# Second products turned to tokens x model columns, expert probabilities applied at the sum, one turn through DRAM

## The chip, the cores and the metric

The kernel runs on one core of a Trainium2 chip. The metric is the device time of one execution in microseconds (us). Before the change the median of three runs is 619.43 us (618.59 to 619.71).

## The reference

Three blocks follow each other: attention with a window (half the heads with a dilated one), a mixture of four experts in which every token uses every expert, and a feed-forward block with a sigmoid gate.

```python
# attention, out: x [1152 tokens, 512]
p = domain_probs / (domain_probs.sum(-1, keepdims=True) + 1e-09)
out = np.zeros((N, D))
for e in range(4):                       # w1[e] 512 x 1024, w2[e] 1024 x 512
    h = np.maximum(x @ w1[e], 0.0)
    out += p[:, e:e + 1] * (h @ w2[e])
x = out
h = x @ w_in                             # 512 x 2048
g = h * (1.0 / (1.0 + np.exp(-1.702 * h)))
return g @ w_out                         # 2048 x 512
```

All inputs and the result are float32.

## The kernel before

Products are run on TensorE (PE) in split precision: each operand is held as a high part and a low part (`xh`, `xl`; `wh`, `wl`), and a product is three matmuls: high x high, high x low, low x high. A matmul takes a stationary operand of 128 x 128 and a moving one of up to 512 columns, and adds into a PSUM bank of 128 x 512 float32. There are eight banks: four of the pool `ps`, four of the pool `pacc`.

The first expert is interleaved with attention by a table of words, SCRIPT. It works in three pieces of 384 tokens and eight tiles f of 128 hidden columns. `F` words are first products (`g1_part`, L521), `h` and `l` write the hidden tile's high and low part, and `2 f i` is a second product (`second`, L563): model columns i x 384 tokens, w2 stationary, the hidden tile moving, 4 values of i with three matmuls each. At f = 7 the sum is multiplied by the expert's probability and goes to `acc` (`g2`, L577), which is laid out model columns x tokens. The probabilities lie along the tokens there, so they have to be repeated on all 128 partitions: `p_turn` (L483) turns them on PE, stores them in DRAM (`pd`) and loads them back with a broadcast.

The other three experts and the gated block run in units s of 256 hidden columns (s = 4 to 15 the experts, 16 to 23 the gated block), each for two groups of tokens c (512 and 640 tokens). `first2` (L790) makes the hidden tile from seven products by a 2 x 2 scheme: the banks a, c, b, d get a product each, then a, c, d a second one. VectorE (DVE) forms `u` and `s` from b and d (L822, L824); the second product into d may start only when L824 has read it. For an expert, DVE then takes the larger of 0 and the value times the probability (`shared`, L839), ScalarE (ACT) writes the high part (L842) and DVE the low part (L852). `second_moe` (L887) is the second product: model columns x tokens, w2 stationary, hidden tile moving; four tiles of 512 tokens for c = 0 (24 matmuls) and eight of 320 tokens for c = 1 (48 matmuls), one DVE add into `acc` each (L919). Units 14 and 15 of c = 1 share one such pass. `second2` (L926), for the gated block, has the other orientation: tokens x model columns, the hidden tile stationary and w2 moving with 512 columns, 24 and 30 matmuls, and a multiply-add on DVE per tile (L946).

The order of units is: first products of (s, 0), second products of (s - 1, 1), first products of (s, 1), second products of (s, 0), and so on. Inside them a table, MID, says which background step is called at each of the places between products. Among these are the rounds that convert the gated block's weights: load a piece `sd` (L727), two ACT steps (L737, L738), two DVE steps into `m` (L743, L747), a GpSimd (POOL) add (L748), and a store of `m` to DRAM (L753). `m` has two buffers, so L743 of a round needs the store of two rounds ago to have landed; `sd` has three. The loads of the weights (`st`, L189) are background steps too. All DMAs are issued by SyncE (SP) in the order of the program: one that has to wait holds all behind it. DVE, ACT, POOL and PE also work in the order of the program.

## Time and profile before

| | |
|---|---|
| median of three runs | 619.43 us |
| the profiled execution's own time | 616.77 us |
| its span | 614.9 us |
| PE busy | 607.6 us, 99% |
| DVE busy | 472.9 us, 77% |
| POOL busy | 358.8 us, 58% |
| ACT busy | 275.9 us, 45% |

The profile is of one execution. The span runs from its first to its last instruction; the execution's own time is 1.9 us longer. Busy time of PE includes the tail of each matmul that overlaps the next one, so what PE does per matmul is read from the starts of matmuls that follow each other, not from the mean duration. An idle engine that nobody waits for costs nothing.

### The profile page before, as it was taken

To read this page: it belongs to the slowest core of one execution; us is meant where nothing else is said; L and a number is where in the kernel's file an instruction comes from. 1 tells how busy PE (TensorE), PEld (TensorE's weight loads), DVE (VectorE), ACT (ScalarE), POOL (GpSimd) and SP (SyncE) were. 2 spreads that over 40 slices of the span, in tenths; PEclk is the share of its full clock that TensorE was granted. 3 is DMA by queue.
4 is the path that set the end of the run, shared out by engine and by line. 5 is a ranking of instruction groups with operands and counts; after the bars stand their busy time and mean duration, and the time that the engine had idled before them with its cause. 6 is when DMAs were issued, how large, how long until landed. Compare 5 with 4: busy or idle time off the path is not lost.

```text
span 614.9 us, 11210 instructions
## 1 busy us (share of the span) xinstructions
PE 607.6 (99%) x4144; PEld 569.2 (93%) x4144; DVE 472.9 (77%) x994; ACT 275.9 (45%) x615; POOL 358.8 (58%) x334
## 2 busy tenths in 40 slices
...
GB/s 319 301 203 154 105 165 177 1 49 122 172 141 134 148 188 151 168 108 170 121 170 176 139 105 170 35 90 72 62 2 103 35 69 36 34 1 1 1 1 154
DMA packets 31446, 69.98 MB, mean 114 GB/s; under 512 B 6908, under 2 KB 12192, under 8 KB 31392
## 3 DMA queue, kind: packets, MB, share of 16 engines
...
q8 instruction: 32, 0.52, 0.4%
...
HBM read 56.26 MB, written 12.99 MB: 113 GB/s over the span
## 4 chain that ended last, share of the span: by engine, by line
PE 93%; DVE 3%; ACT 2%; DMA 1%; issue 1%; SPq 0%; DVEq 0%; ACTq 0%
PE gd L805 10%; PE gc L805 10%; PE ga L805 10%; PE g L539 8%; PE q L909 8%; PE q L911 8%; PE q L910 8%; PE q L939 5%; PE q L937 5%; PE q L938 5%; PE gb L805 5%; PE pa L573 3%; PE pa L575 3%; PE pa L574 3%; DMA pT01small<-home01small 1%
## 5 line engine op out<-in xcount | busy, mean ns | idle before, releaser
L909 PE MATMUL q<-h,w2l 128*128 128x320 f32 (+1 forms) x288 | 97.3, 338 | 0.1
L911 PE MATMUL q<-h,w2h 128*128 128x320 f32 (+1 forms) x288 | 97.2, 338 | 0.0
L910 PE MATMUL q<-h,w2h 128*128 128x320 f32 (+1 forms) x288 | 97.2, 337 | 0.0
L852 DVE TENSOR_TENSOR h<-cc,h 128x256 fp32r<-128x256 f32 (+1 forms) x80 | 74.0, 925 | 20.2 <-ACT h L842 12.5
L748 POOL TENSOR_TENSOR m<-m,sd 128x512 int32<-128x512 int32 x32 | 49.1, 1533 | 62.2 <-ACT h L842 36.8
L692 POOL TENSOR_TENSOR wsl<-ss,wsh 128x512 fp32r<-128x512 f32 x39 | 59.5, 1531 | 31.1 <-ACT wsh L691 31.1
L919 DVE TENSOR_TENSOR acc<-q,acc 128x512 f32<-128x512 f32 (+1 forms) x132 | 70.2, 546 | 9.6 <-PE q L911 8.5
L842 ACT ACTIVATE h<-cc 128x256 fp32r<-128x256 f32 (+3 forms) x48 | 33.0, 687 | 97.3 <-DVE cc L839 96.9
L827 POOL TENSOR_TENSOR cc<-s,u 128x256 f32<-128x256 f32 (+1 forms) x38 | 33.5, 882 | 59.9 <-DVE s L824 59.9
L911 PEld LDWEIGHTS q<-h,w2h 128*128 128x128 f32 x288 | 54.1, 188 | 4.4
L909 PEld LDWEIGHTS q<-h,w2l 128*128 128x128 f32 x288 | 54.1, 188 | 4.0 <-DVE acc L919 0.3
L910 PEld LDWEIGHTS q<-h,w2h 128*128 128x128 f32 x288 | 54.1, 188 | 3.9
L703 POOL TENSOR_TENSOR w2l<-st,w2h 128x512 fp32r<-128x512 f32 x37 | 54.1, 1475 | 5.3 <-ACT w2h L702 4.9
L939 PE MATMUL q<-w2h,h 128*128 128x512 f32 (+1 forms) x146 | 56.9, 390 | 0.0
L937 PE MATMUL q<-w2h,h 128*128 128x512 f32 (+1 forms) x146 | 56.7, 389 | 0.0
L938 PE MATMUL q<-w2l,h 128*128 128x512 f32 (+1 forms) x146 | 56.6, 388 | 0.0
L946 DVE SCALAR_TENSOR_TENSOR acc<-q,acc 128x512 f32<-128x512 f32 (+1 forms) x64 | 42.5, 677 | 11.5 <-PE q L939 11.1
L688 POOL TENSOR_TENSOR wal<-st,wah 128x512 fp32r<-128x512 f32 (+1 forms) x38 | 47.1, 1244 | 2.3 <-ACT wah L687 2.3
L805 PE MATMUL ga<-xh,wal 128*128 128x256 f32 (+1 forms) x160 | 47.3, 296 | 0.0
L805 PE MATMUL ga<-xl,wah 128*128 128x256 f32 (+1 forms) x160 | 47.3, 296 | 0.0
L805 PE MATMUL ga<-xh,wah 128*128 128x256 f32 (+1 forms) x160 | 47.2, 295 | 0.0
L839 DVE SCALAR_TENSOR_TENSOR cc<-cc,pb 128x256 f32<-128x256 f32 (+3 forms) x48 | 42.3, 882 | 1.0
...
## 6 DMA issues: line engine op xcount, KB each, us to landing
...
```

What stands on the lines that cost most here:

```text
L539: nc.tensor.matmul(pt[:, :C], w[:, kt, fs], xx[:, kt, c * C:(c + 1) * C], start=first and y == 0, stop=not todo and y == len(products[x]) - 1)
L692: fns.append(lambda x=x, dst=dst: engine(f"p.{s}.{x}").tensor_tensor(out=sl[:, dst], in0=sums[:, dst], in1=sh[:, dst].bitcast(F32), op=ALU ...
L703: fns.append(lambda o=o: engine(f"q.{s}.{2 * o + 1}").tensor_tensor(out=lo[:, o], in0=t[:, o], in1=hi[:, o].bitcast(F32), op=ALU.subtract))
L805: nc.tensor.matmul(bank_[:, :n], wz[:, y, m, :], xz, start=start and m == 0 and z == 0, stop=m == 1 and z == 2, skip_group_check=not start)
L852: nc.vector.tensor_tensor(out=hl[:, sub], in0=cc[:, sub], in1=hh[:, sub].bitcast(F32), op=ALU.subtract)
L909: nc.tensor.matmul(pt, wl[:, o, cols], hi, start=first, stop=False, skip_group_check=both)
L910: nc.tensor.matmul(pt, wh[:, o, cols], hi, start=False, stop=False, skip_group_check=both)
L911: nc.tensor.matmul(pt, wh[:, o, cols], lo, start=False, stop=last, skip_group_check=both)
L919: nc.vector.tensor_tensor(out=dst[:, on], in0=pt[:, on], in1=src[:, on], op=ALU.add)
L937: nc.tensor.matmul(pt, hi, wh[:, o, cols], start=o == 0, stop=False)
L938: nc.tensor.matmul(pt, hi, wl[:, o, cols], start=False, stop=False)
L939: nc.tensor.matmul(pt, lo, wh[:, o, cols], start=False, stop=o == 1)
```

## The change

The second products of the first expert and of units 4 to 13 get the orientation of `second2`: tokens x model columns, hidden tile stationary, w2 moving with 512 columns (`second`, `second_rows`). A tile of 128 tokens then has its probability on its own partition, so it is a factor per partition in the DVE step that adds to `acc` (or that writes it, for the first expert), and `shared` falls away for units 4 to 13; ACT writes the high part directly with Relu, and DVE the low part with a maximum and a subtraction (`relu_hi`, `relu_lo`). `p_turn` and all broadcast loads but those of the last expert go.

Units 14 and 15 keep the old orientation, so `acc` has to be turned between them. In unit 13 the multiply-add writes back into the PSUM bank, DVE transposes the bank in blocks of 32 x 32 into `acc`, four DMAs per tile write it to a DRAM tensor `turned` in runs of 32 floats (128 bytes), and `back` loads it, turned, for each token group. That is 9 transposes, 36 stores and 2 loads.

PSUM has five banks of `ps` and three of `pacc` up to the end of the first expert, four and four after it.

In SCRIPT the words `2 f 3` and `Z` go and no other word moves.

```diff
...
-F 4 6 7, T 10, W 3 1, F 5 1 2, F 5 3 4, F 5 0 1, 2 0 0, F 4 0 1, L 11, h 1, 2 0 3, D, O 1 1 p 1, 2 0 2, N 14 P,
...
-r 23, C 13 a, C 8 v, V 11, V 15, C 11 v, t 21, C 15 v, R 11, R 13, R 15, R 8, 2 6 0, 2 6 2, F 8 0 1, Z, 2 6 1,
...
+F 4 6 7, T 10, W 3 1, F 5 1 2, F 5 3 4, F 5 0 1, 2 0 0, F 4 0 1, L 11, h 1, D, O 1 1 p 1, 2 0 2, N 14 P, F 3 5 6, l 1,
...
+R 11, R 13, R 15, R 8, 2 6 0, 2 6 2, F 8 0 1, 2 6 1, F 13 2 3, F 9 1 2, F 8 3 4, F 8 4 5, F 11 1 2, A 19, A 17, A 16,
...
@@ -145,19 +144,19 @@
...
     wa = ctx.enter_context(tc.tile_pool(name="wa", bufs=1))
-    ps = ctx.enter_context(tc.tile_pool(name="ps", bufs=4, space=bass.MemoryType.PSUM))
-    pacc = ctx.enter_context(tc.tile_pool(name="pacc", bufs=1, space=bass.MemoryType.PSUM))
+    banks = ExitStack()
+    ps = banks.enter_context(tc.tile_pool(name="ps", bufs=5, space=bass.MemoryType.PSUM))
+    pacc = banks.enter_context(tc.tile_pool(name="pacc", bufs=1, space=bass.MemoryType.PSUM))
     dram = ctx.enter_context(tc.tile_pool(name="dram", bufs=1, space=bass.MemoryType.DRAM))
...
     wr = first_expert.enter_context(tc.tile_pool(name="wr", bufs=4, side=RIGHT))
-    pb0 = first_expert.enter_context(tc.tile_pool(name="pb0", bufs=2, side=RIGHT))
...
     pw = const.tile([P, NC * NTI, E], F32, name="pw")
-    pd = dram.tile([E, NT], F32, name="pd")
+    pd = dram.tile([1, NT], F32, name="pd")
     pwe = const.tile([P, E, NC * NTI], F32, name="pwe")
@@ -171,10 +170,6 @@
...
-
-    def acc_parts(k, a, b):
-        return [(acc_c[c][:, k, max(a, t0) - t0:min(b, t1) - t0], max(a, t0) - a, min(b, t1) - a)
-                for c, (t0, t1) in enumerate(TOK) if max(a, t0) < min(b, t1)]
@@ -480,20 +475,6 @@
...
-    def p_turn():
-        pt = ps.tile([P, 512], F32, tag="ps", name="p_t")[:E * NC * NTI, :P]
-        nc.tensor.transpose(pt, pwe.rearrange("p e t -> p (e t)"), ident)
-        pws = pb0.tile([P, C], F32, tag="pb0", name="pws")[:E * NC * NTI, :P]
-        nc.scalar.activation(pws, pt, AF.Copy)
-        nc.sync.dma_start(out=pd.rearrange("e (t p) -> (e t) p", p=P), in_=pws)
-        for c in range(2):
-            pbe[c] = load_p(pb0, 0, c * C, (c + 1) * C, "pb0")
-
-    def load_p(pool, e, a, b, tag):
-        t = pool.tile([P, b - a], F32, tag=tag, name=f"{tag}_{e}{a}")
-        nc.sync.dma_start(out=t, in_=pd[e:e + 1, a:b].to_broadcast([P, b - a]))
-        return t
-
@@ -558,30 +539,27 @@
...
-    pbe = {}
-
...
         for i in tiles:
-            cols = slice(i * P, (i + 1) * P)
             if f == 0:
...
             wh, wl = wt[s0 + s, 1]
-            t = hbuf[c, f]
-            out_ = pa[i][:, :C]
-            nc.tensor.matmul(out_, wh[:, o, cols], t[:, 0, :], start=f == 0, stop=False)
-            nc.tensor.matmul(out_, wl[:, o, cols], t[:, 0, :], start=False, stop=False)
-            nc.tensor.matmul(out_, wh[:, o, cols], t[:, 1, :], start=False, stop=f == F1 - 1)
-
-    def g2(e, c, f, tiles=range(KT)):
-        if f == 0 and c == 2:
-            pbe[c] = load_p(pb0, e, c * C, (c + 1) * C, "pb0")
+            hi, lo = (hbuf[c, f][:, y, i * P:(i + 1) * P] for y in range(2))
+            nc.tensor.matmul(pa[i], hi, wh[:, o, :], start=f == 0, stop=False)
+            nc.tensor.matmul(pa[i], hi, wl[:, o, :], start=False, stop=False)
+            nc.tensor.matmul(pa[i], lo, wh[:, o, :], start=False, stop=f == F1 - 1)
+
+    def g2(e, c, f, tiles=range(NTI), eng="v"):
         second(4 * e, c, f, f"_{e}{c}", tiles)
...
             for i in tiles:
-                for dst, lo_, hi_ in acc_parts(i, c * C, (c + 1) * C):
-                    nc.vector.tensor_tensor(out=dst, in0=pa[i][:, lo_:hi_], in1=pbe[c][:, lo_:hi_], op=ALU.mult)
+                t = NTI * c + i
+                if eng == "a":
+                    nc.scalar.activation(acc[:, t, :], pa[i], AF.Copy, scale=pwe[:, e, t:t + 1])
+                else:
+                    nc.vector.tensor_scalar_mul(acc[:, t, :], pa[i], pwe[:, e, t:t + 1])
@@ -591,6 +569,7 @@
...
     S0 = SM - 1
+    ROWS_S = range(NF, 14)
     HOLD = ((4, 1), (15, 0), (18, 0),)
@@ -771,6 +750,9 @@
...
+    def nothing():
+        pass
+
@@ -832,7 +814,7 @@
...
         parts_ = ((slice(0, 1), a[:, :n].unsqueeze(1)), (slice(1, 4), cc[:, 1:4]))
-        p_ = late["share"][c].rearrange("p (x n) -> p x n", x=2) if moe else None
+        p_ = late["share"][c].rearrange("p (x n) -> p x n", x=2) if moe and s not in ROWS_S else None
         th = None if moe else late[big].tile([P, 4, n], F32, tag=big, name=f"th{nm}")
@@ -851,14 +833,20 @@
...
-        steps_ = (upper, gate_lo) if moe else (gate, gate_hi, gate_lo)
-        if moe:
+        def relu_hi(sub, src):
+            nc.scalar.activation(hh[:, sub], src, AF.Relu)
+
+        def relu_lo(sub, src):
+            nc.vector.scalar_tensor_tensor(hl[:, sub], src, 0.0, hh[:, sub].bitcast(F32), op0=ALU.max, op1=ALU.subtract)
+
+        steps_ = (relu_hi, relu_lo) if s in ROWS_S else (upper, gate_lo) if moe else (gate, gate_hi, gate_lo)
+        if p_ is not None:
             shared(slice(0, 1), parts_[0][1], slice(0, 1))
...
         nc.vector.tensor_tensor(out=cc[:, 1], in0=c_[:, :n], in1=u2, op=ALU.add)
-        if moe:
+        if p_ is not None:
             shared(slice(1, 2), cc[:, 1:2], slice(1, 2))
@@ -866,17 +854,43 @@
...
         if moe:
-            def share_rest():
-                shared(slice(2, 4), cc[:, 2:4], slice(0, 2))
-                if s % NF == NF - 1 and s < S0:
-                    shares(s // NF + 1, c)
-            rest.insert(0, share_rest)
+            rest.insert(0, nothing if p_ is None else lambda: shared(slice(2, 4), cc[:, 2:4], slice(0, 2)))
         deferred.extend(rest)
...
+
+    turned = {c: dram.tile([KT, P, 2 * N_[c]], F32, name=f"turned{c}") for c in range(2)}
+    STEPS = ((1, 3, 5, 7), (0, 2, 3, 4, 5, 7, 8, 9))
+
+    def second_rows(s, c, slots):
+        n = N_[c]
+        h = hbuf2[s, c]
+        wh, wl = wt[s, 1]
+        for i, t in enumerate(TILES[c]):
+            pt = some_bank(False, f"q{s}_{t}")
+            for o in range(2):
+                hi, lo = (h[:, y, o * 2 * n + i * P:o * 2 * n + (i + 1) * P] for y in range(2))
+                nc.tensor.matmul(pt, hi, wh[:, o, :], start=o == 0, stop=False)
+                nc.tensor.matmul(pt, hi, wl[:, o, :], start=False, stop=False)
+                nc.tensor.matmul(pt, lo, wh[:, o, :], start=False, stop=o == 1)
+                if o == 1:
+                    dst = acc[:, t, :]
+                    to = pt if s == ROWS_S[-1] else dst
+                    nc.vector.scalar_tensor_tensor(to, pt, pwe[:, s // NF, t:t + 1], dst, op0=ALU.mult, op1=ALU.add)
+                    if s == ROWS_S[-1]:
+                        nc.vector.transpose(dst, pt)
+                        home = turned[c].rearrange("k (b y) n -> y (k b) n", y=32)
+                        for a in range(KT):
+                            nc.sync.dma_start(out=home[:, :, i * P + 32 * a:i * P + 32 * a + 32],
+                                              in_=dst[32 * a:32 * a + 32].rearrange("y (b x) -> y b x", x=32))
+                if 2 * i + o in STEPS[c]:
+                    slots()
+
+    def back(c):
+        nc.sync.dma_start(out=acc_c[c], in_=turned[c].rearrange("k p n -> p k n"))
@@ -962,9 +976,8 @@
...
         "l": lambda it: g1_lower(*seq[it][1:]),
-        "2": lambda it, i: g2(*seq[it][1:], tiles=[i]),
+        "2": lambda it, i, eng="v": g2(*seq[it][1:], tiles=[i], eng=eng),
         "w": p_weights,
-        "Z": p_turn,
         "D": lambda: nc.sync.dma_start(out=pw, in_=dp.rearrange("p (t e) -> p t e", e=E)),
@@ -1000,15 +1013,17 @@
...
     first_expert.close()
+    banks.close()
+    ps = ctx.enter_context(tc.tile_pool(name="ps2", bufs=4, space=bass.MemoryType.PSUM))
+    pacc = ctx.enter_context(tc.tile_pool(name="pacc2", bufs=1, space=bass.MemoryType.PSUM))
     words = ExitStack()
...
-    def shares(e, c):
-        late["share"][c] = load_p(late["pb"], e, *TOK[c], f"pb{c}")
-
-    for c in range(2):
-        shares(1, c)
+    nc.sync.dma_start(out=pd.rearrange("e (t p) -> p (e t)", p=P), in_=pwe[:, E - 1, :])
+    for c, (a, b) in enumerate(TOK):
+        late["share"][c] = late["pb"].tile([P, b - a], F32, tag=f"pb{c}", name=f"pb{c}")
+        nc.sync.dma_start(out=late["share"][c], in_=pd[:, a:b].to_broadcast([P, b - a]))
     for nm, n in (("cv", 2), ("sd", 3)):
@@ -1064,9 +1079,6 @@
...
-    def nothing():
-        pass
-
@@ -1129,6 +1141,10 @@
...
             first2(s, c, run or slots)
+            if s == ROWS_S[-1] + 1:
+                back(c)
+        elif s in ROWS_S:
+            second_rows(s, c, run or slots)
         elif s < SM:
...
         else:
```

Two places show what moves. On SP, around the second products of unit 13 (`turned` are the new stores, `acc<-turned` the loads back, `w<-m` the stores of the conversion rounds, `sd` and `st` their loads and those of weights; a trailing xN counts equal rows). Before:

```order
L753 DMA w_60_116<-m_4464 128x512
L727 DMA sd_4604<-in_w_in_dram 128x1024
L753 DMA w_61_117<-m_4566 128x512
L727 DMA sd_4707<-in_w_out_dram 128x1024
L189 DMA st_16_4796<-w_00_104 128x1024
L189 DMA st_16_4798<-w_01_105 128x1024
L753 DMA w_61_117<-m_4647 128x512
L727 DMA sd_4835<-in_w_out_dram 128x1024
L753 DMA w_70_118<-m_4746 128x512
```

and now:

```order
L732 DMA w_60_113<-m_4124 128x512
L706 DMA sd_4237<-in_w_in_dram 128x1024
L887 DMA turned_117<-acc 32x16x32 x12
L732 DMA w_61_114<-m_4199 128x512
L887 DMA turned_117<-acc 32x16x32 x4
L706 DMA sd_4357<-in_w_out_dram 128x1024
L893 DMA acc<-turned_117 128x4x512
L887 DMA turned_118<-acc 32x16x32 x8
L184 DMA st_16_4449<-w_00_101 128x1024
L184 DMA st_16_4451<-w_01_102 128x1024
L732 DMA w_61_114<-m_4278 128x512
```

The store of round 26 (`m_4566` before, `m_4199` now) stands behind twelve new stores, and that of round 27 (`m_4647`, now `m_4278`) behind sixteen, a load back and eight more.

On DVE, from the first products of (14, 0) into the second products of (13, 1) (`u` and `s` are the two sums of `first2`, `m` the first step of round 28, `q` the banks of the second products). Before:

```order
L822 TENSOR_TENSOR u_14_0_4698<-gb_0_4694,s_14_0_4696 128x256
L824 TENSOR_TENSOR s_14_0_4699<-gd_0_4695,s_14_0_4697 128x256
L743 TENSOR_SCALAR m_4746<-sd_4553 128x512
L684 TENSOR_TENSOR ss_4725<-st_15_4514 128x256
L839 SCALAR_TENSOR_TENSOR cc_0_4700<-ga_0_4692,pb_30_3969 128x256
L852 TENSOR_TENSOR h_0_4749<-cc_0_4700,h_0_4749 128x256
L860 TENSOR_TENSOR cc_0_4700<-gc_0_4693,u_14_0_4698 128x256
L839 SCALAR_TENSOR_TENSOR cc_0_4700<-cc_0_4700,pb_30_3969 128x256
L866 TENSOR_TENSOR cc_0_4700<-gd_0_4695,u_14_0_4698 128x256
L919 TENSOR_TENSOR acc<-q_100_4770,acc 128x320
L919 TENSOR_TENSOR acc<-q_110_4778,acc 128x320
L747 SCALAR_TENSOR_TENSOR m_4746<-sd_4553,m_4746 128x512
```

and now:

```order
L804 TENSOR_TENSOR u_14_0_4348<-gb_0_4344,s_14_0_4346 128x256
L806 TENSOR_TENSOR s_14_0_4349<-gd_0_4345,s_14_0_4347 128x256
L722 TENSOR_SCALAR m_4396<-sd_4190 128x512
L663 TENSOR_TENSOR ss_4375<-st_15_4164 128x256
L821 SCALAR_TENSOR_TENSOR cc_0_4350<-ga_0_4342,pb_1841 128x256
L834 TENSOR_TENSOR h_0_4399<-cc_0_4350,h_0_4399 128x256
L848 TENSOR_TENSOR cc_0_4350<-gc_0_4343,u_14_0_4348 128x256
L821 SCALAR_TENSOR_TENSOR cc_0_4350<-cc_0_4350,pb_1841 128x256
L854 TENSOR_TENSOR cc_0_4350<-gd_0_4345,u_14_0_4348 128x256
L882 SCALAR_TENSOR_TENSOR q_4_4421<-q_4_4421,pwe,acc 128x512
L884 STREAM_TRANSPOSE acc<-q_4_4421 128x512
L726 SCALAR_TENSOR_TENSOR m_4396<-sd_4190,m_4396 128x512
```

The steps of `first2` and of the round stand as before; each tile of the second products now brings a multiply-add of 512 columns and a transpose in place of an add of 320.

## Rows read from the trace of the kernel before

**Rows 1.** The page: busy time of each engine, then shares of the chain of waits.
```profile
PE 607.6 (99%) x4144; PEld 569.2 (93%) x4144; DVE 472.9 (77%) x994; ACT 275.9 (45%) x615; POOL 358.8 (58%) x334
...
PE 93%; DVE 3%; ACT 2%; DMA 1%; issue 1%; SPq 0%; DVEq 0%; ACTq 0%
```

**Rows 2.** Chain of waits in order of time: start us, length us, what.
```profile
236.22 0.88 PE ga L805 x6
...
260.04 0.88 PE ga L805 x6
...
522.57 0.88 PE ga L805 x6
...
546.13 0.88 PE ga L805 x6
```

**Rows 3.** The same chain in the gated block, second products of c = 0.
```profile
552.29 0.24 PE q L937
...
557.80 0.70 PE ga L805 x6
```

**Rows 4.** The same chain in the first expert.
```profile
106.66 2.10 PE g L539 x12
...
127.54 2.08 PE g L539 x12
```

**Rows 5.** DVE groups by line and shape: xcount, busy us, mean ns, idle before.
```profile
L946 DVE SCALAR_TENSOR_TENSOR acc<-q,acc 128x512 f32<-128x512 f32 x62 | 41.7, 685 | 11.2 <-PE q L939 10.8
L919 DVE TENSOR_TENSOR acc<-q,acc 128x320 f32<-128x320 f32 x86 | 39.8, 482 | 7.9 <-PE q L911 7.3
L919 DVE TENSOR_TENSOR acc<-q,acc 128x512 f32<-128x512 f32 x44 | 29.5, 678 | 1.7 <-PE q L911 1.2
...
L363 DVE STREAM_TRANSPOSE tr12big<-prob12big 96x512 f32<-96x512 f32 x2 | 1.4, 703 | 1.2 <-POOL prob12big L347 1.2
```

**Rows 6.** Busy time by stretch: us, PE, PEld, DVE, ACT, POOL, clock, DMA, GB/s.
```profile
361.50:379.50 18.00, 17.95 (x116) 16.61 (x116) 16.51 (x29) 6.73 (x13) 10.67 (x9) 1.00 0.48 138
```

**Rows 7.** DVE in order of time, units 13 and 14: start us, us, line, operation.
```profile
363.77 0.67 DVE L919 TENSOR_TENSOR acc<-q,acc 128x512 f32<-128x512 f32 x1
364.37 0.81 DVE L839 SCALAR_TENSOR_TENSOR cc<-cc,pb 128x640 f32<-128x640 f32 x1
...
370.52 0.48 DVE L743 TENSOR_SCALAR m<-sd 128x512 uint32<-128x512 uint32 x1
370.92 1.51 DVE L684 TENSOR_TENSOR ss<-st 128x256 f32<-128x256 f32 x1
...
380.73 0.41 DVE L684 TENSOR_TENSOR ss<-st,ss 128x256 f32<-128x256 f32 x1
381.06 0.41 DVE L743 TENSOR_SCALAR m<-sd 128x512 uint32<-128x512 uint32 x1
...
383.39 0.48 DVE L824 TENSOR_TENSOR s<-gd,s 128x320 f32<-128x320 f32 x1
```

**Rows 8.** Chain of waits in order of time, units 13 and 14.
```profile
361.48 0.23 PE q L909
...
379.46 0.87 PE ga L805 x6
```

**Rows 9.** SP's DMA issues in order of time, unit 13.
```profile
359.56 0.42 SPq L753 DMA_DIRECT2D w<-m  x1
```

**Rows 10.** SP's issues in attention: stores of turned tiles of 32 x 4 x 128.
```profile
79.71 2.85 SPq L372 DMA_DIRECT2D home12big<-tr12big  x6
```

**Rows 11.** The tile m: its stores' time from issue to landing.
```profile
DMA to landing us min/median/max: 2.0/4.4/7.4
```

**Rows 12.** Who waited for whom, DVE: total us, times, longest us.
```profile
DVE m L743 <- DMA w<-m: 0.7, 1, 0.7
```

**Rows 13.** DMA issues: xcount, KB each, median us to landing.
```profile
home13big<-tr13big SPq DMA_DIRECT2D x6, 64.0 KB, 1.8
...
home10big<-tr10big SPq DMA_DIRECT2D x8, 36.0 KB, 1.6
```

More of the change, by code (lines that the diff above doesn't have):

```diff
@@ L105 @@
-F 14 1 2, 2 10 2, 2 11 2, V 19, V 23, t 16, F 14 5 6, C 23 a, F 15 6 7, 2 12 2, t 17, K 14, r 21, C 19 v, F 14 4 5,
-F 15 4 5, F 15 5 6, 2 10 3, F 15 1 2, 2 11 3, 2 10 0, F 15 7 8, r 17, 2 10 1, 2 11 1, 2 11 0, 2 12 0, 2 12 1, h 15,
-2 12 3, r 16, r 20, R 19, R 23, V 17, V 21, h 14, 2 13 3, 2 13 1, 2 13 0, 2 13 2, l 14, C 21 v, C 17 a, R 21, R 17,
-l 15
+F 4 6 7, T 10, W 3 1, F 5 1 2, F 5 3 4, F 5 0 1, 2 0 0, F 4 0 1, L 11, h 1, D, O 1 1 p 1, 2 0 2, N 14 P, F 3 5 6, l 1,
+H 1 1 1, O 1 1 p 0, K 7, O 0 1 v 3, A 9, H 3 0 0, 2 1 2, F 5 6 7, r 12, H 2 1 0, N 9 p, O 3 0 p 0, T 23, T 14, 2 1 0,
@@ new lines @@
+F 3 6 7, 2 0 1, F 4 3 4, Q 22, U 9, N 11 V, c 9 v, H 3 1 0, F 4 2 3, F 3 3 4, 2 1 1, F 5 5 6, 2 2 1, F 3 0 1, F 3 4 5,
+t 10, T 11, O 3 1 v 1, t 23, K 13, t 14, O 2 1 p 1, O 2 1 v 0, 2 2 0, H 3 0 1, S 21, h 5, h 4, S 13, h 3, A 22,
+H 3 1 1, O 3 0 p 3, t 11, r 10, K 6, r 14, O 3 0 p 2, O 1 1 p 2, O 3 0 p 1, l 5, K 5, O 1 1 p 3, S 15, S 8, S 20,
+O 3 1 p 2, l 3, l 4, V 12, F 7 3 4, Q 21, H 2 1 1, Q 13, F 7 1 2, Q 15, L 12, F 7 6 7, 2 3 0, N 22 v, A 13, F 7 7 8,
+N 13 p, F 6 4 5, C 12 a, R 12, A 15, Q 8, F 6 2 3, N 15 v, O 3 1 v 0, T 13, F 7 5 6, 2 3 1, T 15, O 2 1 p 2, A 21,
@@ new lines @@
+O 2 1 p 3, N 21 P, F 7 0 1, 2 2 2, A 8, 2 4 1, F 7 2 3, N 8 v, F 6 3 4, F 6 1 2, F 6 6 7, T 22, Q 20, F 7 4 5,
+F 6 5 6, F 6 7 8, t 13, O 3 1 p 3, 2 3 2, h 7, F 6 0 1, l 7, t 15, V 14, t 22, h 6, V 9, K 9, C 14 a, V 10, r 15, w,
+C 9 a, A 20, C 10 a, 2 4 2, 2 4 0, S 18 19, R 14, S 16 17, R 9, 2 5 2, l 6, R 10, U 8, T 21, Q 18, K 11, 2 5 1, A 18,
+Q 16, Q 19, Q 17, 2 5 0, N 20 V, c 8 a, r 13, r 11, V 13, V 8, r 23, C 13 a, C 8 v, V 11, V 15, C 11 v, t 21, C 15 v,
+R 11, R 13, R 15, R 8, 2 6 0, 2 6 2, F 8 0 1, 2 6 1, F 13 2 3, F 9 1 2, F 8 3 4, F 8 4 5, F 11 1 2, A 19, A 17, A 16,
@@ new lines @@
+F 9 2 3, F 9 5 6, F 8 5 6, F 8 1 2, F 8 7 8, F 9 0 1, F 13 5 6, F 8 2 3, N 18 p, F 9 4 5, K 15, r 22, F 11 5 6,
+F 8 6 7, F 13 7 8, N 17 p, h 8, F 11 6 7, 2 7 0, l 8, F 9 6 7, F 11 4 5, 2 7 1, T 17, F 13 1 2, T 20, F 11 3 4,
+F 9 7 8, F 13 0 1, F 12 0 1, F 9 3 4, F 11 2 3, F 12 5 6, h 9, l 9, T 18, t 20, F 12 6 7, F 12 1 2, F 12 3 4,
+F 10 2 3, F 10 7 8, N 19 P, F 11 0 1, T 19, 2 7 2, F 10 3 4, 2 8 1, F 13 4 5, F 11 7 8, F 10 5 6, F 13 6 7, F 10 0 1,
+F 10 1 2, F 12 2 3, F 10 6 7, F 10 4 5, F 12 7 8, N 16 P, h 11, t 18, t 19, 2 8 0, 2 8 2, F 12 4 5, 2 9 1, h 10, T 16,
@@ L109 @@
+2 9 0, l 10, l 11, F 13 3 4, F 14 2 3, K 12, 2 9 2, F 14 6 7, h 13, h 12, F 15 0 1, F 14 0 1, r 19, F 14 7 8,
+F 15 3 4, l 13, F 14 3 4, F 15 2 3, l 12, r 18, F 14 1 2, 2 10 2, 2 11 2, V 19, V 23, t 16, F 14 5 6, C 23 a,
+F 15 6 7, 2 12 2, t 17, K 14, r 21, C 19 v, F 14 4 5, F 15 4 5, F 15 5 6, F 15 1 2, 2 10 0, F 15 7 8, r 17, 2 10 1,
+2 11 1, 2 11 0, 2 12 0, 2 12 1, h 15, r 16, r 20, R 19, R 23, V 17, V 21, h 14, 2 13 1, 2 13 0, 2 13 2, l 14, C 21 v,
+C 17 a, R 21, R 17, l 15
 """
```

17 lines of the change are left out of this document (removed).

## The prediction

> **What bounds the kernel now.** I read the page's busy times first, then the chain of waits, then the chain piece by piece, and went to single engines only where the chain leaves PE. PE is busy for 99% of the span and carries 93% of the chain; DVE, the next engine on it, has 3% [rows 1]. So a matmul taken away counts in full, and a cost elsewhere counts only where it makes PE wait. The place to look for that is found by the same rule read backwards: in the 18 us from 361.5 to 379.5, which are the second products of unit 13 and the first products of (14, 0), DVE is busy for 16.5 us while its average is 77% [rows 1, 6]. The granted clock there is 1.00, that is 2.4 GHz.
>
> **What the second products give.** The number of columns that PE streams does not change: 24 matmuls of 512 stay 24 of 512, 48 of 320 become 30 of 512, and in the first expert 12 of 384 become 9 of 512 per hidden tile. What changes is the cost per matmul and per orientation. The kernel already holds both orientations, so the gain can be read off. A unit of the experts takes from one first product of c = 1 to the next 260.04 - 236.22 = 23.82 us, a unit of the gated block, with the same first products and with the new orientation, 546.13 - 522.57 = 23.56 us [rows 2]. That is 0.26 us for each of ten units: 2.6 us.
>
> For the first expert, five rounds of 24 matmuls of 384 columns (12 first products, 12 second) take 127.54 - 106.66 = 20.88 us, 174.0 ns each, 2.088 us for twelve [rows 4]. In the new orientation 24 matmuls of 512 take 557.80 - 552.29 = 5.51 us, 229.6 ns each, 2.066 us for nine [rows 3]. The difference of 0.022 us comes 24 times: 0.5 us. The PE transpose of the probabilities is one instruction, which I price at nothing. Sum of the gains: 3.1 us.
>
> A matmul of 384 columns is 160 ns at 2.4 GHz, so the rows show 14 ns above the columns, and that is what fewer matmuls save. The Trainium skill (TensorE: Matmul & The Clock Gate, section Back-to-back issue gap) gives 2.5 ns above the columns for isolated matmuls; by that the 18 matmuls fewer per unit and 72 fewer in the first expert would give 252 times 2.5 ns, an estimate of 0.6 us, and the median would be 624.1. This trace has 14 ns wherever such matmuls follow each other, so I keep 3.1, and that result gets no chance of its own.
>
> **What costs nothing.** In units 4 to 12 DVE loses the three products with the probability per token group and gets multiply-adds for adds: 685 ns for 678 at 512 columns, five times 685 for eight times 482 at c = 1 [rows 5], so it has less to do, and nobody waits. ACT reads Relu from a bank where it copied from a tile: as many instructions, and a bank of `first2` is next written only after a full second product. The broadcast loads of `pd` vanish from SP; the new store of 1,152 single floats and its two loads come before unit 4 and are first read in unit 14. Five banks instead of four in the attention part may free a wait or two; PE is idle for 7.3 us of the whole span [rows 1], and I give this nothing, at most 1 us.
>
> **What unit 13 costs on DVE.** I follow DVE from the first tile of (13, 0) to the sum `s` of (14, 1), since PE's seventh product of (14, 1) may not start before `s` is read. Before, that is 363.77 to 383.39 + 0.48 = 383.87 [rows 7]. Added: nine multiply-adds of 685 ns and nine transposes. The trace has no transpose of 128 x 512 from a bank, the nearest is 96 x 512 from a tile, 703 ns [rows 5]; 478 (an add of 320 columns) and 950 would be wide ends, 9 times 0.25 us either way, and I take 703 since the columns are the same. Together 9 x 1.388 = 12.5 us. Removed: four adds of 678, eight of 482, and the 640-wide product with the probability at 364.37, 0.81 us [rows 5, 7]: 7.4 us. So DVE has 5.1 us more. It can begin 0.7 us sooner: six matmuls after 361.48 [rows 8], at 229.6 ns, the first bank is done at 362.9, about 363.05 with its tail. It also fills some of the 1.5 us in which it idled [rows 6], I take 0.8. `s` is then read by 383.87 + 5.1 - 0.7 - 0.8 = 387.5. PE, left alone, begins the first products of (14, 1) at 379.46 [rows 8] and the seventh of them six times 0.88 us later, at 384.7, less the 0.25 gained in unit 13: 384.5. PE waits 3.0 us.
>
> One piece of this is soft: the `ss` step at 370.92 took 1.51 us where the other of its line and width, at 380.73, took 0.41 [rows 7], so what stood in its way need not do so again: 1.1 us less if not.
>
> **What unit 13 costs through SP.** Thirty-six stores go into SP's queue, each waiting for its transpose, and the stores of `m` wait behind them. An issue costs SP about 0.47 us, by 2.85 us for six turned tiles in attention [rows 10]. The store of round 26 went out at 359.56 [rows 9]; now it follows the third tile of (13, 0). That transpose ends near 367.8 (363.05, then 1.39 us per tile and one step of 0.6 for `m` between), its four issues end at 369.7, and the store lands 2.0 to 4.4 us after its issue, minimum and median [rows 11]: at 371.7 to 374.1. The first step of round 28, which takes that buffer, stood at 370.52 [rows 7] and would now stand at 370.8. So DVE waits 0.9 to 3.3 us, with all the sums of (14, 0) and the tiles of (13, 1) behind it. I take 1.5, near the short end, because the two weight loads that used to lie around this time are held up behind the same stores and leave the queue empty. The same again one round later: the store of round 27 now follows the second tile of (13, 1), near 380.5, eight issues and two weight loads of which four issues and both loads fall after it: out at 383, landed 385 to 387.4, wanted at 381.06 [rows 7] plus the 5.3 us by which DVE is then late, 386.4. That is 0 to 1.0 us, I take 0.5. That such a wait bites is in the trace: once, for 0.7 us, DVE already waited for it [rows 12].
>
> The turn itself is covered: `acc` of c = 0 is wanted only in the second products of (14, 0), after 389; its last transpose ends near 369.2, four issues, a landing of about 2 us [rows 13] and the load back bring it to about 378. The second turn is wanted some 20 us after its last store.
>
> After (14, 1) DVE runs with less lead than it had; I add 0.3 us for that.
>
> **The sum.** Waits 3.0 + 1.5 + 0.5 + 0.3 = 5.3 us, gains 3.1, so 2.2 us slower. The profiled execution took 616.77 us, 1.9 more than its span of 614.9; it becomes 619.0. The median of the runs shown lies 2.7 us above that execution, so the median becomes 621.6.
>
> **The rivals.**
>
> No change. The stores land at the short end and find the buffers in time, `ss` takes its 0.4 us, and what is left of the 3.0 us wait equals the gain: -0.9 to +1.2 us, 618.5 to 620.6. For it: one soft step of 1.1 us and a wait whose lower end is near nothing. Against: DVE must do 5 us more in a stretch with 1.5 us idle.
>
> Faster. If PE's wait in unit 13 is below 1.8 us, the change wins: at none, 616.3. It decides at the seventh product of (14, 1). For it: DVE comes to unit 13 with the products with the probability taken off it, and other steps of that stretch may run quicker once POOL is less in their way; the extra bank. Against: the sum above begins at the first bank's end, so an emptier queue before it does not help.
>
> The turn's stores are dear. The pieces are 128 bytes, 512 to a store, where attention's have 384 or 512 bytes and at most 128 to a store. Attention's stores land in 1.6 and 1.8 us [rows 13] with no sign of a price per piece. If a store with four times the pieces took SP four times as long, 1.9 us, the 16 of c = 0 would end near 394 and the 20 of c = 1 near 432, with the load back of c = 1 some 20 us after it is wanted: about 640. The Trainium skill (DMA: Bandwidth & Descriptors, section Specifications) has pieces under 512 bytes done as read-modify-write, which would speak for this one; the 384-byte stores here land no later than the 512-byte ones, so at that size the trace does not show it.
>
> The change does not do what it says: then PE's row counts stay; the order shows otherwise, and I give it no chance.
>
> **Chances.** Forecast, slower by 0.8 to 6 us: 0.52. No change: 0.22. Faster: 0.20. Dear stores: 0.06. About 0.2% (1.2 us) is what a measurement of this kernel can tell from no change; by that slower has 0.58, the same 0.22, faster 0.20. The forecast's own range is 620.0 to 625. For eight in ten I take 617.5, which leaves out the lower half of the faster case, to 628.5, which takes in stores that cost some microseconds more than priced.
>
> **What would show it.** The units of the experts should come every 23.56 us, and unit 4 should begin 0.5 us earlier than before. In unit 13 DVE should show nine pairs of multiply-add and transpose of about 0.69 and 0.70 us with little idle between, two idle pieces of DVE before the first step of `m` put down to the store of `m`, and PE one wait of 3 to 6 us before the seventh product of (14, 1), released by DVE. If PE's waits there are under 1.8 us in all, the step on DVE's load was wrong; if a store's issue takes much over 0.5 us or DVE waits for the load back, the step on the turn was wrong; if the units still take 23.8 us, the gain was.

## The result

The changed kernel takes 627.55 us (median of 4 runs, 627.14 to 628.87), the kernel before, run beside it, 619.01 us (617.44 to 619.71). The ratio is 1.0145, 95% interval 1.0120 to 1.0171: it is slower, by 8.5 us where 2.2 were forecast. The forecast had the direction and the place right and the size wrong: the time lies outside the forecast's own 620.0 to 625 and near the upper end of the wider range, 617.5 to 628.5.

The page of the profiled execution (627.14 us, span 625.4) shows where to look. PE has 253 matmuls fewer than in [rows 1], and yet it is busy for 0.7 us more and for 97% of the span in place of 99%.

```profile
PE 608.3 (97%) x3891; PEld 547.4 (88%) x3891; DVE 438.1 (70%) x906; ACT 274.3 (44%) x614; POOL 344.6 (55%) x334
...
PEclk9999999999999999999999998899999999999999
...
PE 89%; DVE 4%; issue 2%; ACT 2%; SPq 1%; DMA 1%; POOL 0%; DVEq 0%; ACTq 0%
```

The third row is the chain: DVE, SP's queue and the DMAs have gained what PE lost [rows 1]. The row between is the granted clock in 40 slices: it dips in slices 25 and 26, 375 to 406 us.

Where the time went is read best from mark to mark, since executions begin the first expert at different times. Marks in the chain of the kernel before, beside 522.57 in [rows 2], and of the kernel after (start us, length us, what):

```profile
98.25 2.09 PE g L539 x12
...
140.94 0.88 PE ga L805 x6
...
355.32 0.88 PE ga L805 x6
```
```profile
97.25 2.08 PE g L520 x12
...
139.56 0.88 PE ga L787 x6
...
163.12 0.88 PE ga L787 x6
...
351.60 0.88 PE ga L787 x6
...
533.00 0.88 PE ga L787 x6
```

From the first expert's rounds to the first products of (4, 1) it is 42.69 us before, 42.31 after: 0.4 won. From there to (13, 1), nine units, 214.38 and 212.04: 2.3 won, and a unit comes every 23.56 us, as in the gated block [rows 2]. From (13, 1) to the same unit of the gated block 167.25 and 181.40: 14.15 us lost. Everything that went wrong lies there.

PE's waits between 340 and 420 us (us in total, times, longest us); the kernel before has 0.3 us in this stretch:

```profile
PE gd L787 <- DVE s L806: 8.2, 3, 7.5
PE ga L787 <- ACT s L798: 1.1, 1, 1.1
PE gb L787 <- DVE cc L848: 1.0, 1, 1.0
PE q L876 <- DVE acc L884: 0.5, 1, 0.5
```

The 7.5 us are the wait that was forecast, in its place if not in its size: the seventh product of (14, 1), for DVE's `s`. DVE in order of time (the brackets hold the idle time before, and what ended it):

```profile
369.92 0.92 DVE L722 TENSOR_SCALAR m<-sd 128x512 uint32<-128x512 uint32 x1 [1.93 <-DMA w<-m]
370.76 0.41 DVE L663 TENSOR_TENSOR ss<-st 128x256 f32<-128x256 f32 x1
...
376.24 0.72 DVE L884 STREAM_TRANSPOSE acc<-q 128x512 f32<-128x512 f32 x1
...
382.27 0.39 DVE L663 TENSOR_TENSOR ss<-st,ss 128x256 f32<-128x256 f32 x1
387.92 0.43 DVE L722 TENSOR_SCALAR m<-sd 128x512 uint32<-128x512 uint32 x1 [5.27 <-issue]
...
390.26 0.48 DVE L806 TENSOR_TENSOR s<-gd,s 128x320 f32<-128x320 f32 x1
...
396.18 0.43 DVE L722 TENSOR_SCALAR m<-sd 128x512 uint32<-128x512 uint32 x1 [2.42 <-DMA w<-m]
```

Three times DVE stands before the first step of `m`, for 1.93, 5.27 and 2.42 us; [rows 12] had 0.7 in the whole run. The 5.27 are put down to nothing (issue), so its cause has to be found at the other end. SP's queue in order of time:

```profile
360.98 6.36 SPq L887 DMA_DIRECT2D turned<-acc  x12
367.39 0.50 SPq L732 DMA_DIRECT2D w<-m  x1
...
374.99 6.12 SPq L887 DMA_DIRECT2D turned<-acc  x8
381.21 0.94 SPq L184 DMA_DIRECT2D st<-w  x2
382.19 0.42 SPq L732 DMA_DIRECT2D w<-m  x1
```

The stores of turned tiles, `turned<-acc`, are called spills from here on. The store of round 26 goes out at 367.4 (at 359.56 in [rows 9], where unit 13 begins 3.7 us later), behind twelve spills. That of round 27 goes out at 382.2, behind eight more and two weight loads; DVE has wanted its buffer since 382.66. From issue to landing (first the two weight loads, then that store):

```profile
DMA to landing us min/median/max: 4.4/4.9/5.4
```
```profile
DMA to landing us min/median/max: 5.6/5.6/5.6
```

So the weight loads land at 385.7 and 387.2 and the store at 387.8, and DVE goes on at 387.92: that wait ends with the store's landing, 5.2 us after the issue ended.

The idle PE then cost a second time. Stretches of 2 us (columns as in [rows 6]), and the chain behind them:

```profile
384.00:386.00 2.00, 0.00 (x0) 0.00 (x0) 0.00 (x0) 0.00 (x0) 0.00 (x0) 1.00 0.97 332
386.00:388.00 2.00, 0.00 (x0) 0.00 (x0) 0.08 (x1) 0.00 (x0) 0.00 (x0) 0.56 1.15 304
388.00:390.00 2.00, 0.00 (x0) 0.00 (x0) 1.97 (x4) 0.00 (x0) 0.79 (x1) 0.50 0.91 141
...
394.00:396.00 2.00, 2.00 (x7) 1.54 (x6) 0.00 (x0) 0.00 (x0) 0.90 (x1) 0.50 0.60 164
396.00:398.00 2.00, 2.00 (x9) 1.63 (x8) 1.82 (x4) 0.00 (x0) 0.00 (x0) 0.88 0.64 133
```
```profile
390.80 1.97 PE gd L787 x6
392.76 0.43 PE q L923
...
396.60 0.23 PE q L923
```

PE is idle from 383.3 to 390.8; the granted clock falls to 0.50, the lower level, while it is, and is still there for its first matmuls. Six matmuls take 1.97 us in place of 0.88, and nine of 512 columns 0.43 in place of 0.23: 1.09 + 9 x 0.20 = 2.9 us. Waits of 10.8 - 0.3 and 2.9 of clock make 13.4 of the 14.15 us lost.

### The profile page after: what moved, and what is told of

Its sections match the earlier page's. It is cut to its first block, busy times and chain, and to the rows that moved or that the text cites. A ratio compares the mean times of both kernels' runs of the same rounds, so it can differ in the third digit from the quotient of the medians.

```text
span 625.4 us, 10674 instructions
## 1 busy us (share of the span) xinstructions
PE 608.3 (97%) x3891; PEld 547.4 (88%) x3891; DVE 438.1 (70%) x906; ACT 274.3 (44%) x614; POOL 344.6 (55%) x334
## 4 chain that ended last, share of the span: by engine, by line
PE 89%; DVE 4%; issue 2%; ACT 2%; SPq 1%; DMA 1%; POOL 0%; DVEq 0%; ACTq 0%
PE gd L787 9%; PE ga L787 9%; PE gc L787 9%; PE g L520 8%; PE q L878 6%; PE q L877 6%; PE q L876 6%; PE q L953 5%; PE q L951 5%; PE q L952 5%; PE gb L787 5%; PE pa L550 3%; PE pa L551 3%; PE pa L552 3%; PE q L924 1%
## 5 line engine op out<-in xcount | busy, mean ns | idle before, releaser
L882 DVE SCALAR_TENSOR_TENSOR acc<-q,pwe,acc 128x512 f32<-128x512 f32 x81 | 60.7, 749 | 35.7 <-PE q L878 35.4
L876 PE MATMUL q<-w2h,h 128*128 128x512 f32 x180 | 70.5, 392 | 0.5 <-DVE acc L884 0.5
L878 PE MATMUL q<-w2h,h 128*128 128x512 f32 x180 | 70.8, 393 | 0.0
L671 POOL TENSOR_TENSOR wsl<-ss,wsh 128x512 fp32r<-128x512 f32 x39 | 53.8, 1386 | 30.5 <-ACT wsh L670 20.2
L877 PE MATMUL q<-w2l,h 128*128 128x512 f32 x180 | 70.4, 391 | 0.0
L798 ACT ACTIVATE s<-ga 128x256 f32<-128x256 f32 (+1 forms) x40 | 16.3, 409 | 66.7 <-PE ga L787 66.7
L667 POOL TENSOR_TENSOR wal<-st,wah 128x512 fp32r<-128x512 f32 (+1 forms) x38 | 42.0, 1110 | 2.3 <-ACT wah L666 2.3
L834 DVE TENSOR_TENSOR h<-cc,h 128x256 fp32r<-128x256 f32 (+3 forms) x40 | 36.3, 908 | 9.4 <-ACT h L831 5.2
L787 PE MATMUL gd<-t,wah 128*128 128x256 f32 (+1 forms) x160 | 34.3, 304 | 8.4 <-DVE s L806 8.4
L876 PEld LDWEIGHTS q<-w2h,h 128*128 128x128 f32 x180 | 33.8, 188 | 7.4 <-DVE acc L884 0.9
L878 PEld LDWEIGHTS q<-w2h,h 128*128 128x128 f32 x180 | 33.8, 188 | 7.3
L877 PEld LDWEIGHTS q<-w2l,h 128*128 128x128 f32 x180 | 33.8, 188 | 6.8
```

The costliest lines, as they stand in the source:

```text
L671: fns.append(lambda x=x, dst=dst: engine(f"p.{s}.{x}").tensor_tensor(out=sl[:, dst], in0=sums[:, dst], in1=sh[:, dst].bitcast(F32), op=ALU ...
L787: nc.tensor.matmul(bank_[:, :n], wz[:, y, m, :], xz, start=start and m == 0 and z == 0, stop=m == 1 and z == 2, skip_group_check=not start)
L876: nc.tensor.matmul(pt, hi, wh[:, o, :], start=o == 0, stop=False)
L877: nc.tensor.matmul(pt, hi, wl[:, o, :], start=False, stop=False)
L878: nc.tensor.matmul(pt, lo, wh[:, o, :], start=False, stop=o == 1)
L882: nc.vector.scalar_tensor_tensor(to, pt, pwe[:, s // NF, t:t + 1], dst, op0=ALU.mult, op1=ALU.add)
```

## The experiments

All edits are to the changed kernel. They ran in four groups (noturn, nodma, cv3n and late_cv3n; dmaonly, split, split_cv3n and ps4; mq and the two p15; best), with the kernel before beside each: 617.97, 617.65, 618.37 and 617.57 us. The last column is free of where an execution begins: the time from the first products of (4, 1) to the marked unit of the gated block (533.00 above), less the 381.63 us of the kernel before. It is of one execution each: ps4, whose program behind the first mark is that of the changed kernel, shows 9.9 us for 11.8, so a difference of 2 us in this column alone tells nothing.

| kernel | median us (runs) | ratio to before, 95% | mark to mark, us |
|---|---|---|---|
| after | 627.55 (4) | 1.0120 to 1.0171 | +11.8 |
| noturn | 614.60 (4) | 0.9933 to 0.9970 | -2.2 |
| nodma | 621.19 (10) | 1.0019 to 1.0056 | +1.6 |
| dmaonly | 628.07 (4) | 1.0143 to 1.0186 | +11.5 |
| cv3n | 622.55 (4) | 1.0050 to 1.0106 | +4.6 |
| late_cv3n | 621.90 (7) | 1.0042 to 1.0075 | +3.6 |
| mq | 627.58 (4) | 1.0119 to 1.0162 | +10.9 |
| split | 629.83 (4) | 1.0180 to 1.0219 | +12.1 |
| split_cv3n | 620.88 (10) | 1.0023 to 1.0062 | +4.1 |
| ps4 | 629.29 (4) | 1.0165 to 1.0211 | +9.9 |
| cv3n_p15 | 622.03 (4) | 1.0043 to 1.0085 | +6.3 |
| split_cv3n_p15 | 617.66 (11) | 0.9968 to 0.9999 | 0.0 |
| best | 616.69 (12) | 0.9981 to 1.0020 | -0.6 |

**A square: transposes and stores, neither, one, the other.** The first kernel takes out the whole turn, the second takes out only its DMAs, the third takes out only the nine transposes (one to a token tile).

```diff
 noturn:  -  to = pt if s == ROWS_S[-1] else dst      +  to = dst
          -  if s == ROWS_S[-1]:  (transpose, spills)  +  if False:
          -  nc.sync.dma_start(out=acc_c[c], in_=turned[c]...)   +  pass
 nodma:   -  nc.sync.dma_start(out=home[...], in_=dst[...])       +  pass
          -  nc.sync.dma_start(out=acc_c[c], in_=turned[c]...)   +  pass
 dmaonly: -  to = pt if s == ROWS_S[-1] else dst      +  to = dst
          -  nc.vector.transpose(dst, pt)
```

> Leaves the turn out of unit 13: no transposes, no stores of turned tiles, no load back (the sums of units 14 and 15 then meet in the wrong layout, so the output is not the reference's). This is the new orientation alone. All theories: PE has no wait in units 13 and 14, the units come every 23.56 us, time about 4 us below the kernel before, 615 us against 619 (unit 13 began 3.7 us earlier in the changed kernel). If the new orientation itself costs something in units 13 to 15, less than that.

> Keeps the nine transposes on DVE and leaves out the 36 stores and the two loads back (output not the reference's). Theory A, the stores in SP's queue hold up the stores of m and DVE waits for those: the wait of 7.5 us before the seventh product of (14, 1) goes, at most 0.5 us of it stays, the granted clock stays at 1.00, 615 to 616 us. Theory B, DVE's own load in unit 13 (the 3.0 us of the prediction): PE still waits 2 to 3 us there, 618 us.

> This kernel leaves out the 45 transposes on DVE (nine pieces of four or five times... nine in all, one to a token tile) and keeps the multiply-adds, the 36 stores and both loads, so that the sums come back unturned. It is the fourth corner of a square: neither 614.6 us, transposes alone 617.9 to 621.8, both 627.5. Theory A (the two stores of m that stand behind the spills on SP's queue): DVE still waits 5 to 7 us in all for its m buffers, PE idles 3 to 6 us for s of the second token group of unit 14, and the time is 619 to 623. Theory B (DVE's own work in units 13 and 14): without 9 x 0.72 = 6.5 us of transposes DVE has slack to wait in, the time is under 616.5 and PE's wait for s under 1 us. Theory C (the two only hurt together, the wait falls on an engine that has no slack left): DVE waits as in A, but PE idles under 2 us, and the time is 615.5 to 618.

Without the turn the change wins 3.4 us. With the transposes alone it loses 3.2. PE's waits between 340 and 420 us in nodma, and the sum they wait for:

```profile
PE gd L787 <- DVE s L806: 2.6, 2, 2.1
PE ga L787 <- ACT s L798: 0.7, 1, 0.7
```
```profile
384.56 0.48 DVE L806 TENSOR_TENSOR s<-gd,s 128x320 f32<-128x320 f32 x1
```

The 7.5 us wait is gone and a wait of 2.1 us stays, as theory B has it. The ten runs of nodma fall into two groups: four with a mean granted clock of 1.00 take 617.9 to 619.3 us (B's 618; the trace is of one of them), six with 0.994 to 0.997 take 621.2 to 621.8, some 3 us more. How much of the 3 us is the clock, and how much a longer wait before it, is not shown, since none of the six was traced.

With the DMAs alone the kernel is as slow as with both, though DVE has 6.5 us less to do. DVE and SP in dmaonly:

```profile
371.63 0.48 DVE L722 TENSOR_SCALAR m<-sd 128x512 uint32<-128x512 uint32 x1 [2.76 <-DMA turned<-acc]
...
389.80 0.43 DVE L722 TENSOR_SCALAR m<-sd 128x512 uint32<-128x512 uint32 x1 [8.83 <-issue]
```
```profile
375.50 7.37 SPq L886 DMA_DIRECT2D turned<-acc  x8
382.97 0.93 SPq L184 DMA_DIRECT2D st<-w  x2
383.95 0.42 SPq L732 DMA_DIRECT2D w<-m  x1
```

The first DVE row names a spill, but the store of `m` issued at 368.81 lands at 371.6, when DVE goes on. In the second row DVE comes to the step earlier and waits 8.83 us in place of 5.27; what it is let go by, the store of round 27, lands as late as in the changed kernel, at 391.3 and 391.6 us in the old trace's time (each shifted by how much earlier its (13, 1) begins). So the store sets the pace, and the transposes only fill the time in which DVE would wait. The two costs are not added, the longer one counts: theory B falls for the whole kernel, and C (that each hurts only with the other) falls too. A's way stands, but not its sizes: DVE waits 14.1 us for `m` where it had 5 to 7, PE 10.1 us for `s` where it had 3 to 6, and the time is 628 us where it had 619 to 623. The square does not part the 36 spills from the two loads back, which noturn and nodma leave out as well; what the loads back cost by themselves stays open.

**A third buffer for `m`.** The third buffer needs room, which one of five buffers of small sums gives (what that costs by itself no run shows); the second kernel also issues a group's spills after its last tile.

```diff
 cv3n:      -  for nm, n in (("cv", 2), ("sd", 3)):   +  (("cv", 3), ("sd", 3))
            -  ("ns", 5)                               +  ("ns", 4)
 late_cv3n: +  the same, and the spills of a group collected in a list and issued after its tiles
```

> The changed kernel with three buffers for m in place of two (paid for by four buffers of the short sums in place of five). The turn is complete. Theory A: the first step of a round waits for the store of three rounds ago, so the waits of 1.9 and 5.3 us go, a wait of up to 2 us may be left at rounds 30 and 31; no fall of the clock; 616 to 618 us. Theory B: 3 us on DVE stay, 621 us. Theory C, the small pieces load the DMA engines and that is what costs: 626 to 628 us, as the changed kernel.

> Three buffers for m as above, and the stores of the turned tiles of one token group put behind the second products of that group, so that the stores of rounds 26 and 27 go ahead of them. Theory A: no wait of DVE for a store before round 31, 615 to 616 us. Theory B: 618 us. Theory C: the same bytes in the same pieces, 626 us.

DVE's waits for `m` fall from 9.6 to 3.4 us in cv3n, and the time above the kernel before from 8.5 to 4.6 us, mark to mark from 11.8 to 4.6. So much is A's part, and C, which had no change, falls; but the time, 622.6, is above A's 616 to 618 and B's 621. In late_cv3n DVE waits for no store at all, PE still waits 2.8 us for `s`, which is DVE's load as in nodma, and the time, 621.9, is again above A's and B's and under C's. One thing that A and B left out is the clock: PE's longest wait, 2.1 us, is as long as in the traced run of nodma, but here the granted clock falls after it (0.50 from 388 to 390 us), where that of nodma stays at 1.00.

**The store of `m` from another queue.** One word: `nc.sync` becomes `nc.scalar` at the store of `m`.

> As the changed kernel, with the store of m alone issued from ACT's queue in place of SP's; the 36 spills stay on SP's. Nothing is left out. It parts two ways in which the spills hold up that store. Theory order (the store waits on SP until the spills ahead of it are issued): it is issued as soon as its data stand, DVE's waits for m fall from 7.2 us to under 2, and the time is 618 to 622. Theory traffic (the store is issued in time, but lands late since 36 stores of small pieces hold the DMA engines): it still takes 4 us or more to land, DVE still waits 4 us or more for m, and the time is over 624.

The wait for the store is gone, as order has it: its median time to landing falls from 4.5 to 2.3 us, and DVE waits on no `w<-m`. The time is that of traffic, for a third reason. SP in mq, ACT, DVE, and one row of the list of what SP waited for:

```profile
398.39 0.44 SPq L706 DMA_DIRECT2D sd<-in_w_out_dram  x1
```
```profile
402.81 0.65 ACT L716 ACTIVATE sd<-sd 128x512 int32<-128x512 uint32 x1 [5.91 <-DMA sd<-in_w_out_dram]
```
```profile
404.03 0.43 DVE L722 TENSOR_SCALAR m<-sd 128x512 uint32<-128x512 uint32 x1 [6.36 <-ACT sd L717]
```
```profile
SPq L887 <- DMA w<-m: 12.7, 2, 7.1
```

The next thing in SP's queue, the load of `sd`, is now late behind the spills, and `m` with it. So whatever stands behind the spills is late, and which item is hit depends on the rest. But mq does not show that SP's order alone costs: the spills are late themselves, by 5.6 us inside the first sixteen and by 7.1 us before the seventeenth, and the list puts both to the store of `m`, now in ACT's queue. Why they wait for it stays open.

**The turn in two units.** The first group's turn goes into unit 12; its unit 13 goes by model columns as before.

```diff
-  ROWS_S = range(NF, 14)
+  LAST = (12, 13)         # s in ROWS_S becomes NF <= s <= LAST[c]
```

> The turn of the first token group is put into unit 12 and that of the second stays in unit 13; the first group's unit 13 goes by model columns as in the kernel before. Nothing is left out. DVE's transposes and SP's 36 stores are spread over two units. Theory A (SP's queue): the store of the second group's round still stands behind up to 20 spills, DVE waits 3 to 6 us for m, the time is 620 to 625. Theory B (DVE's work in unit 13): four of nine transposes and 16 of 36 stores leave the tight place, the time is 616 to 619. If neither holds it stays at 627.

> As the split turn, with three buffers for m in place of two (and four in place of five for the small sums, to make room). Nothing is left out. If A and B together are the whole of the loss, DVE waits under 2 us for m, PE idles under 1.5 us for s of unit 14, the clock stays at 1.0, and the time is 615 to 617, below the kernel before (618.0). If something else costs (the transfers' traffic, the turned order's other costs), it stays above 618.

The time is neither theory's number for split, and even above the 627 us of neither: with two buffers each turn has its own late DMA, and the sum is no smaller. SP and DVE at the first turn:

```profile
352.49 0.97 SPq L184 DMA_DIRECT2D st<-in_w_dram  x2
353.51 0.64 SPq L736 DMA_DIRECT2D w<-m  x1
```
```profile
361.09 0.43 DVE L726 TENSOR_SCALAR m<-sd 128x512 uint32<-128x512 uint32 x1 [4.75 <-ACT sd L720]
```

The store issued at 353.5, again behind two weight loads, lands at 361.0; the step of ACT that the row names ends at 361.0 too, so the trace does not tell which of the two ended the wait. With three buffers DVE waits 3.2 us for a store at the first turn, where it has slack and PE waits for nothing, but PE still waits 2.1 us for `s` of (14, 1): above 618, as the second branch had it.

**The banks in attention.** `bufs=5` becomes 4.

> As the changed kernel, but with four shared banks in place of five in the attention part, as the kernel before had. Nothing is left out. It asks where the first part's gain of 1.4 us (0.5 forecast) comes from. Theory bank: unit 4's first product begins 0.7 to 1.0 us later than in the changed kernel (140.3 to 140.6 us in place of 139.56). Theory expert: the gain is all in the first expert's second products, and it begins at 139.5 to 139.7. The total would move by as much, or by nothing that can be told.

Both theories fall. Unit 4 begins at 142.35, but the first expert does too: its rounds begin at 100.03 here (97.25 above), and from there to (4, 1) it is 42.32 us, as with five banks. The traced executions with five banks begin these rounds anywhere from 97.25 to 100.90 (late_cv3n). Behind the mark the fifth bank shows no effect, and what it does ahead of it is lost in that spread; of the 1.4 us by which unit 4 begins sooner, 0.4 are gain after that mark, and most of the rest is an earlier start.

**DVE's own steps moved away.** Three steps of unit 15's weights go to POOL, without and with the split; the last kernel also moves background steps of unit 14, two of them DVE steps of `m`, behind `s`.

```diff
 cv3n_p15, split_cv3n_p15:  -  BY_VECTOR = ("p.15.2", "p.15.3", "p.15.9", "p.16.0",
                            +  BY_VECTOR = ("p.16.0",
 best, unit 14 alone:       -  ("1", 1): "d w p.4 | w p.5 | d w |  | p.10 | p.6 q.2 | w p.11 w | "
                            +  ("1", 1): "d p.4 | p.5 | d |  | w p.10 | w p.6 q.2 | w p.11 w w | w"   (and one w less at the end of ("2", 1))
```

> As the changed kernel with three buffers for m, four for the small sums (622.6 us), and three steps of the weights of unit 15 (two sums and one subtraction, 0.96, 0.38 and 0.65 us on DVE in the stretch from 370 to 385) on POOL in place of DVE. Nothing is left out. If what was left there is DVE's load, the 2.0 us taken from it come off PE's waits: s of unit 14 waits under 2 us in all in place of 4.4, and the time is 619 to 621. If it is the stores, nothing moves: 622 to 623.

> As the split turn with three buffers for m, four for the small sums (620.9 us), and the same three steps of unit 15's weights on POOL in place of DVE. Nothing is left out. If both causes are met, PE's wait for s of unit 14 falls from 2.9 us to under 1, the clock stays at its upper level, and the time is 615.5 to 617.5, under the kernel before (617.8). If POOL becomes late for unit 15's weights, PE waits there instead and the time is 619 to 621.

> As the split turn with three buffers for m and unit 15's three steps on POOL (617.7 us), and in unit 14 two steps of m (0.39 and 0.70 us on DVE, just ahead of the steps on which PE waited 1.4 us) stand behind these steps in place of ahead of them. Nothing is left out. If that wait of 1.4 us is DVE's load alone, it falls to under 0.5 us and the time is 616 to 617, under the kernel before by 0.2 to 0.4%. If the steps moved only delay the next ones, it stays at 617.5 to 618.5.

In cv3n_p15 DVE has 2 us less to do and waits 4.8 us for the stores in place of 3.4; PE's wait for `s` does not fall, it is 6.3 us for 4.4, and the time stays (622.0 for 622.6). As in dmaonly: where the store sets the pace, work taken off DVE buys nothing. In the split, where it does not, it buys 4.1 us mark to mark, and 3.9 us of the time above the kernel before. PE's wait for `s` there between 330 and 430 us, and in the whole of best:

```profile
PE gd L791 <- DVE s L810: 1.9, 2, 1.4
```
```profile
PE gd L791 <- DVE s L810: 1.6, 4, 0.7
```

split_cv3n_p15 is at the kernel before, 0.16% under it with an interval that nearly touches 1. best's longest wait falls from 1.4 to 0.7 us (under 0.5 was asked), its median is 0.9 us under the kernel before, but the ratio's interval, 0.9981 to 1.0020, holds 1. One interval of thirteen that ends at 0.9999 is no proof: no complete version is shown to beat the kernel before. noturn's 614.6 us says what there was to win.

## Why the prediction missed the size

**The gain of 3.1 us: right.** 2.34 us for nine units is the 0.26 each, and the first expert won 0.4 after the mark at 98.25 and 0.2 before it (63.84 to 98.25 before, 63.01 to 97.25 after). The tenth unit, 13, shows none: noturn takes 0.15 us longer than before from (13, 1) on. So about 2.9.

**DVE's load, 3.0 us of wait: near, for a kernel without the stores.** `s` was to be read at 387.5 in the old trace's time. nodma has read it at 384.56 + 0.48 = 385.04 and begins (13, 1) 2.87 us earlier, 352.45 for 355.32: 387.9. PE waits 2.1 us for it, and 0.5 and 0.7 us for two sums of unit 14 before it, 3.3 in all. The parts were near too: multiply-add and transpose took 740 and 717 ns (forecast 685 and 703), and the soft `ss` step 0.96 us in nodma and 0.41 in the changed kernel, not 1.51. Forms of DVE in the changed kernel (count, busy us, mean ns, idle before):

```profile
L882 DVE SCALAR_TENSOR_TENSOR q<-q,pwe,acc 128x512 f32<-128x512 f32 x9 | 6.7, 740 | 0.0
L884 DVE STREAM_TRANSPOSE acc<-q 128x512 f32<-128x512 f32 x9 | 6.5, 717 | 0.3
```

**"The store of round 27 ... out at 383, landed 385 to 387.4, wanted at 386.4 ... I take 0.5": the step that failed.** In the old trace's time (add 355.32 - 351.60 = 3.72), DVE wanted it at 382.66 + 3.72 = 386.4, as forecast, and the second tile's transpose ended at 376.96 + 3.72 = 380.7, where 380.5 was forecast. What was sized too small is what comes behind it. From that transpose to the end of the store's issue it took 5.6 us (376.96 to 382.61) in place of 2.5: SP was still issuing the first tile's spills, and then the first of the second tile's four took 2.01 us where an issue mostly takes 0.5:

```profile
377.47 2.01 SPq L887 DMA_DIRECT2D turned<-acc  x1
```

It ends at 379.5, just before the load back of the first group lands (issued at 372.89, 6.8 us to landing). Such an issue stands at the same place in dmaonly (2.33 us) and in ps4 (2.46); what holds it is not shown. So the issue of the store ended at 386.3 in place of 383. It then landed 5.2 us later, where I had taken 2.0 to 4.4 from a stretch in which the DMA engines were half busy [rows 6, 11]; here they were at 0.8 to 1.15, and of the two weight loads just ahead of it the second landed only 0.6 us before it. A wait of 5.27 us for 0.5.

One round earlier SP had already fallen behind: four spills take it 2.1 us, and DVE brought the tiles 1.4 and 2.0 us apart, so the store of round 26 was out at 367.89 + 3.72 = 371.6 where 369.7 was forecast. That wait came out near, 1.93 us for 1.5.

**The store after that** was not priced: 2.42 us more. In all DVE waited 9.6 us for `m` where 2.0 were forecast.

**The sum added what does not add.** 3.0 for DVE's work and 2.0 for its waits were put on top of each other. Against noturn, which has neither, the transposes alone cost 3.8 us mark to mark, the DMAs alone 13.7, both 14.0 (by the medians, each against the kernel before beside it, 6.6, 13.8 and 11.9): they lie side by side. By itself that would have made the forecast too high; the size of the store's wait outweighed it.

**The clock** had no term: 2.9 us, after an idle stretch of 7.5 us.

**The rivals.** Faster and no change fell at the place where they were to be decided. Dear stores fell in the form given: an issue mostly costs SP about 0.5 us (12 in 6.36), a few cost 1 to 2.5, where this rival had 1.9 for each. Nor do the small pieces land late by themselves. The median of all 36 spills is 3.0 us where attention's 64 KB take 1.8 [rows 13], but that is not so for the first twelve, which have nothing large ahead of them. Their median from issue to landing, and their stretch, 360.5 to 367 us (packets, MB, share of the DMA engines):

```profile
turned<-acc SPq DMA_DIRECT2D x12, 64.0 KB, 2.0
```
```profile
q1 hardware_dynamic: 4956, 0.62, 60.3%
```

The later ones land behind the load back and the weight loads. What the pieces do cost is time of the DMA engines: 60% of it for 95 GB/s here, 48% for 138 GB/s in [rows 6], by an estimate from these two stretches about 1.8 times as much for a byte. The Trainium skill (DMA: Bandwidth & Descriptors, section Specifications) has pieces under 512 bytes done as read-modify-write; the direction agrees, and no run here shows what is done inside.
